# w_mod's load as two 64-row halves, one on SyncE's queue and one on ScalarE's

## The chip, the core and the metric

The kernel runs on one core of a Trainium2 chip. The core has a matrix engine (TensorE, PE in the profile; its weight loads are PEld), VectorE (DVE), ScalarE (ACT), GpSimd (POOL) and SyncE (SP), which here only issues transfers. Transfers between the chip's memory (HBM) and the core's on-chip memory of 128 rows (partitions) run on 16 DMA engines. The metric is device time in microseconds (us), the median of several runs.

## What is computed

One token of 640 numbers, x, goes through a transformer block with adaptive layer norm. A vector c gives six modulation vectors: silu(c) times w_mod, a matrix of 640 x 3840. Then comes attention with a cache of 32 heads, 16,384 keys and values of 128 numbers for each, and then a gated feed-forward layer. All arrays are bf16.

```
mod = (silu(c) @ w_mod).reshape(1, 6, 1, 640)
sa, ca, ga, sb, cb, gb = six rows of mod
h = layernorm(x) * (1 + ca) + sa
q = h @ wq                      # 32 heads of 128
p = softmax(q k^T / sqrt(128))  # 16384 keys a head
x = x + ga * ((p v) @ wo)
h = layernorm(x) * (1 + cb) + sb
x = x + gb * ((silu(h @ w_gate) * (h @ w_up)) @ w_down)
```

Nearly all bytes are the two caches, 16 pairs of heads with 8.39 MB of keys (K) and as much of values (V) each. w_mod has 4.92 MB and wq 5.24 MB; the whole input is 290.5 MB.

## The kernel before, in words

The kernel is a list of operations, each with an engine, a position (a number that sorts the operations of one engine), and the operations that it depends on. A small planner (lines 38 to 180) sorts each engine's list by position and writes it out. An engine works its list strictly in order; before an operation it waits on the semaphores of those that it depends on. Transfers are operations too (line 71): one instruction on an engine that issues it, by default SyncE, and a semaphore that is raised when the transfer has landed. Transfers that one engine issues stand in one queue.

**On-chip memory.** One large buffer, `big`, has three slots of 65,536 bytes a row. w_mod lies in slot 2 and wq in slot 1 (lines 237 and 238) until they are used up; K of pair 0 goes to slot 0, K of pair 1 to slot 1, V to slot 2. So K of pair 1 may be loaded only when the q matmuls have read all of wq (line 485), and V of pair 0 only when the w_mod matmuls are done (line 615).

**The queues at the start.** SyncE issues w_mod (line 327), wq (line 328), K of pair 0 in two halves of 4.19 MB (line 484), then K of pair 1 and V of pair 0, and from there on a K and a V for each turn of the loop over pairs, each waiting for its slot to come free. ScalarE issues c and x (lines 325 and 326), 1,280 bytes each. `w_mod.rearrange("(p k) n -> p k n", p=128)` puts five rows of w_mod side by side into each on-chip row, so an on-chip row takes 38,400 contiguous bytes.

**What uses them.** In PE's order: c is turned into columns (line 344), then x (line 345); VectorE and ScalarE make silu(c) (lines 348 to 351). PE makes the sums of the layer norm (lines 370 and 377), the partition number from a ramp that VectorE writes after `xn` (lines 353 to 361), x in chunks (line 346), and then the rows of the modulation (`mod_rows`, line 405): for shift and scale (line 415), and for five further banks (line 423), three of them before the first q matmul. VectorE picks columns out of them (`take`, line 398) and makes `h_col` (line 422). The q matmuls (lines 435 to 457) run in eight groups, each copied out by ScalarE (line 450).

**The loop over pairs.** VectorE multiplies K by q in place (line 627), folds halves together (line 640), and sums (line 642) to get the scores; ScalarE makes the exponentials (line 562); PE multiplies them with V (line 578). In the last pair PE takes over an eighth of the scores. At the end come wo, the second layer norm, and the feed-forward layer, whose weights are loaded in the slots that are free by then (lines 662 to 703).

Of the kernel before, what the change touches and what calls it, by code (L numbers as in the profile page):

```python
# [37 lines left out]
class _Plan:  # L38
# [21 lines left out]
    def op(self, eng, pos, fn, deps=(), name="", chan=None, turn=None):  # L60
        o = _Op(eng, pos, fn, list(deps), name, len(self.ops))
        o.turn = turn
        if chan is not None:
            if chan not in self.chans:
                self.chans[chan] = _Chan(self.es.enter_context(self.nc.semaphore("ch_" + chan)), 1)
            o.chan = self.chans[chan]
            o.sig = True
        self.ops.append(o)
        return o
# [113 lines left out]
def build(nc, A_x, A_k, A_v, A_wq, A_wo, B_wg, B_wu, B_wd, c_in, w_mod, out):  # L183
# [33 lines left out]
    with es:  # L217
        block = es.enter_context(nc.Block())
        plan = _Plan(nc, es)
# [15 lines left out]
        def mat(n, o, k, cols):  # L235
            return slot(n)[:, o:o + k * cols].rearrange("p (k n) -> p k n", k=k)
        wm_v = mat(2, 0, KC, 6 * D)
# [76 lines left out]
        ACT, DVE, PE = "act", "dve", "pe"  # L314
        op = plan.op
# [7 lines left out]
        wm_src = w_mod.rearrange("(p k) n -> p k n", p=128)  # L323
        wq_src = A_wq.rearrange("(p k) n -> p k n", p=128)
        d_c = plan.dma(0.06, c_one, c_in, "c", name="dma_c", eng="act")
        d_x = plan.dma(0.07, x_one, A_x[0], "x", name="dma_x", eng="act")
        d_wm = plan.dma(0.0, wm_v, wm_src, "wm", name="dma_wmod")
        d_wq = plan.dma(0.1, wq_v, wq_src, "wq", name="dma_wq")


# [20 lines left out]
        o_sc = op(DVE, 0.5, lambda e: e.tensor_tensor(out=silu_c[:], in0=c_col, in1=rr[:], op=ALU.mult), deps=[o_rr], name="silu_c")  # L351
# [3 lines left out]
        while n < 128:  # L355
            o_rp = op(DVE, 1.3 + 0.001 * n, lambda e, n=n: e.tensor_scalar_add(out=ramp[:, n:2 * n], in0=ramp[:, 0:n], scalar1=float(n)),
                      deps=[o_rp], name="ramp%d" % n)
            n *= 2
        o_pc = op(PE, 1.5, lambda e: e.matmul(A_ps[:, 0:1], lhsT=ramp[0:1, :], rhs=one_f[0:1, 0:1], start=True, stop=True),
                  deps=[o_rp, o_onesf], name="partition_number")  # L360
        o_pn = op(DVE, 1.6, lambda e: e.tensor_copy(out=on_f[:, 0:1], in_=A_ps[:, 0:1]), deps=[o_pc], name="partition_number_sb")
        o_ident = op(DVE, 1.7, lambda e: e.tensor_scalar(out=ident[:], in0=ramp, scalar1=on_f[:, 0:1], scalar2=None, op0=ALU.is_equal),
                     deps=[o_pn], name="ident")
# [41 lines left out]
        def mod_rows(pos, dst, c0, c1, deps, name):  # L405
            def f(e):
                last = None
                for a in range(c0, c1, 512):
                    b = min(a + 512, c1)
                    for kd in range(KC):  # L410
                        last = e.matmul(dst[:, a - c0:b - c0], lhsT=silu_c[:, kd:kd + 1].broadcast_to([128, 128]), rhs=wm_v[:, kd, a:b],  # L411
                                        start=(kd == 0), stop=(kd == KC - 1))
                return last
            return op(PE, pos, f, deps=[d_wm, o_sc] + deps, name=name)
        for m, (wide, free) in enumerate(((psw[3], o_rstd), (psw[2], o_pn))):
            o_m = mod_rows(2.0 + 0.01 * m, wide, m * D, (m + 1) * D, [free], "mod_rows%d" % m)
            for k in range(KC):
                take(2.05, wide[:, k:D:KC], moda[:, m * KC + k:m * KC + k + 1], o_m)
        o_t1 = op(DVE, 2.1, lambda e: e.scalar_tensor_tensor(
            out=tt1[:], in0=moda[:, KC:2 * KC], scalar=1.0, in1=xn[:], op0=ALU.add, op1=ALU.mult),  # L420
            deps=[o_take[-1], o_xn], name="t1")
        o_h = op(DVE, 2.2, lambda e: e.tensor_tensor(out=h_col[:], in0=tt1[:], in1=moda[:, 0:KC], op=ALU.add), deps=[o_t1], name="h_col")
        mod_banks = [6, 7, 4, 5, 2]
        for i, bk in enumerate(mod_banks):
            late = i >= 3
            o_mod_b = mod_rows((2.52 if late else 2.4) + 0.001 * i, psb[bk], 2 * D + 512 * i, 2 * D + 512 * (i + 1), [o_take[2 * KC - 1]], "mod_rows_b%d" % i)
            for c in range(4):
                o_modc = take(BU(0) + 4.2 if late else 2.42, psb[bk][:, 128 * c:128 * (c + 1)], modb[:, 4 * i + c:4 * i + c + 1], o_mod_b)
# [182 lines left out]
        for u in range(NU):  # L611
# [13 lines left out]
            for c, (a, b) in enumerate(zip(cuts, cuts[1:])):  # L625
                qb = qbc[:, u].unsqueeze(1).broadcast_to([128, b - a, 128])
                prev.append(op(DVE, B + (13.0 if u == 0 else 4.5) * c, lambda e, ks=ks[:, a:b, :], qb=qb: e.tensor_tensor(out=ks, in0=ks, in1=qb, op=ALU.mult),  # L627
                               deps=[d_k[u][c if u == 0 else 0], o_qbc[u]], name="mult%d_%d" % (u, c)))
# [9 lines left out]
            while w > 16:  # L638
# [4 lines left out]
                          deps=prev + ([o_exp[u - 1]] if u else []) + [o_xs.get(u)], name="red%d" % u)  # L643
            o_max[u] = op(DVE, E - 0.5, lambda e, u=u: e.tensor_reduce(out=pm[:], in_=S_v[:], axis=AX.X, op=ALU.max),  # L644
                          deps=[o_red[u], o_row[u - 1] if u else None], name="max%d" % u, chan="max")
# [56 lines left out]
        for a in range(2 * NP2, FCH):  # L702
# [5 lines left out]
                  deps=[o_abf, o_modc], name="ga_attn")  # L708
        o_x1 = op(DVE, TE + 0.2, lambda e: e.scalar_tensor_tensor(
            out=x1, in0=tt2[:], scalar=1.0, in1=x_res[:], op0=ALU.mult, op1=ALU.add, accum_out=st[:, 4:5]),  # L710
            deps=[o_ga, o_xf1], name="x1")
# [3 lines left out]
            deps=[o_xc1, o_rstd1, o_onep_b], name="t2")  # L715
        o_h2 = op(DVE, TE + 1.1, lambda e: e.tensor_tensor(out=h2_col[:], in0=tt3[:], in1=sb_, op=ALU.add),
                  deps=[o_t2], name="h2_col")
# [5 lines left out]
        def f_hrow(e):  # L723
            last = None
            for c in range(KC):
# [5 lines left out]
                   deps=[o_hr], name="h2_row1")]  # L731
# [34 lines left out]
        for i, (a, b) in enumerate(zip(WD_CUTS, WD_CUTS[1:] + [FCH])):  # L766
# [13 lines left out]
            deps=[prev, o_gbx, o_x1, o_zf], name="out_pairs")  # L780
# [9 lines left out]
def bass_adaLN_cond__gqa_block_cached__swiglu_ffn__decode_kernel(  # L790
    nc: bass.Bass,
    A_x: bass.AP,
    A_k_cache: bass.AP,
    A_v_cache: bass.AP,
    A_wq: bass.AP,
    A_wo: bass.AP,
    B_x: bass.AP,
    B_w_gate: bass.AP,
    B_w_up: bass.AP,
    B_w_down: bass.AP,  # L800
    c: bass.AP,
    w_mod: bass.AP,
    out: bass.AP,
):
    build(nc, A_x, A_k_cache, A_v_cache, A_wq, A_wo, B_w_gate, B_w_up, B_w_down, c, w_mod, out)
# [28 lines left out]
```

## Time and profile before

| | us |
|---|---|
| median of 3 runs (lowest and highest) | 681.05 (680.98 to 681.2) |
| the profiled execution | 681.08 |
| its span, from first to last instruction | 679.2 |
| VectorE busy in the span | 613.4 |
| TensorE busy in the span | 172.2 |
| ScalarE busy in the span | 59.7 |
| bytes moved by DMA, mean rate | 290.61 MB, 428 GB/s |

The profile is one execution of the kernel, as the hardware's profiler recorded it. A page of it gives busy times, the span cut into 40 slices with a digit for the busy share of each engine in tenths, the queues, and the costliest groups of instructions. The trace behind it can be asked further. A row of its timeline reads: start, duration (both us), engine, line of the kernel, operation, what is written <- what is read, how many; then in brackets the time for which the engine had been idle before, and what ended that. SPq and ACTq are instructions by which SyncE and ScalarE issue transfers; their duration is that of the issue and not of the transfer. For every packet that a DMA engine moved the trace has a record with queue, start, duration and bytes; a table of queues adds them up.

| issues at the start | issued at us | KB | us from issue to landing |
|---|---|---|---|
| w_mod, SyncE | 0.73 | 4800 | 14.1 |
| c, ScalarE | 0.76 | 1.2 | |
| wq, SyncE | 1.20 | 5120 | 26.1 |
| x, ScalarE | 1.31 | 1.2 | |
| K of pair 0, two halves, SyncE | 1.65 on | 4096 each | 40.4 (median) |

### The profile page before, as it was taken

The page shows a single profiled execution, that of the slowest core. Times are in us where ns is not written, and L with a number is a line of the kernel's source. Part 1 is how long each engine was busy: PE and PEld are TensorE (multiplying, and loading weights), DVE is VectorE, ACT ScalarE, POOL GpSimd, SP SyncE. Part 2 cuts the span into 40 slices and gives each one's busy share as a digit, 9 for nine tenths or more (in the row PEclk, how much of TensorE's full clock was granted, in tenths as well). Part 3 has the DMA queues.
Part 4 walks back from the last instruction along what each step waited for, and adds up shares of the span by engine and source line. Part 5 has one row for each costly group of instructions (what it writes and reads, how often), then busy time and mean ns, then how long its engine had stood idle before and what let it go on. Part 6 is the DMA issues. An engine that isn't in the chain of part 4 may idle for free.

```text
span 679.2 us, 4346 instructions
## 1 busy us (share of the span) xinstructions
PE 172.2 (25%) x1840; PEld 85.9 (13%) x1840; DVE 613.4 (90%) x250; ACT 59.7 (9%) x203; POOL 0.2 (0%) x4
## 2 busy tenths in 40 slices
PE   2720040404013030403103040301204030213465
PEld 1300010201001010201001010100101010102244
DVE  2389999999999999999999999999999999999801
ACT  1120100101010100101010100001010100003110
POOL 0000000000000000000000000000000000000000
PEclk9975565755557575655757565565756565566675
DMA  9999999999999999999999999999999999999996
GB/s 384 429 458 432 432 432 436 432 432 432 432 433 432 432 432 432 432 432 432 432 432 436 429 432 432 432 436 432 432 432 432 432 432 436 432 436 438 423 422 280
DMA packets 6936, 290.61 MB, mean 428 GB/s; under 512 B 716, under 2 KB 910, under 8 KB 1678
## 3 DMA queue, kind: packets, MB, share of 16 engines
q1 hardware_dynamic: 6922, 290.48, 99.1%
q8 instruction: 6, 0.10, 0.1%
q14 instruction: 4, 0.03, 0.0%
q10 hardware_dynamic: 4, 0.00, 0.0%
HBM read 290.47 MB, written 0.00 MB: 428 GB/s over the span
## 4 chain that ended last, share of the span: by engine, by line
DVE 80%; DMA 14%; issue 3%; SPq 2%; PE 0%
DVE big L627 35%; DVE big L640 33%; DMA big<-in_A_k_cache_dram 11%; DVE S_v L642 10%; DMA big<-in_B_w_down_dram 3%; SPq L78 2%; DVE big L630 1%; DVE gm L548 0%; DVE pm L644 0%; DVE on_f L595 0%; DVE kt L400 0%; PE psw L772 0%; DVE acc_sb L400 0%; DVE psw L488 0%; DVE S_v L400 0%
## 5 line engine op out<-in xcount | busy, mean ns | idle before, releaser
L627 DVE TENSOR_TENSOR big<-big,qbc 128x8192 bf16<-128x8192 bf16 (+3 forms) x32 | 275.5, 8610 | 13.1 <-DMA big<-in_A_k_cache_dram 13.1
L640 DVE TENSOR_TENSOR big<-big 128x8192 bf16<-128x8192 bf16 (+5 forms) x47 | 236.0, 5021 | 1.6
L578 PE MATMUL psw<-big,P 128*8 128x512 bf16 x1024 | 90.2, 529 | 114.4 <-DMA big<-in_A_v_cache_dram 114.4
L545 PE MATMUL psw<-ident_f,pm 128*1 128x128 f32 x32 | 9.4, 396 | 267.4 <-DVE pm L644 267.4
L642 DVE TENSOR_REDUCE S_v<-big 128x256 f32<-128x4096 bf16 (+1 forms) x16 | 70.2, 4387 | 0.5
L578 PEld LDWEIGHTS psw<-big,P 128*8 128x8 bf16 x1024 | 29.3, 111 | 168.6 <-DMA big<-in_A_v_cache_dram 111.7
L545 PEld LDWEIGHTS psw<-ident_f,pm 128*1 128x1 f32 x32 | 1.4, 80 | 269.2 <-DVE pm L644 269.2
L558 ACT ACTIVATE nb<-psw 128x1 f32<-128x1 f32 x16 | 2.7, 171 | 361.0 <-PE psw L555 361.0
L582 ACT ACTIVATE acc_sb<-psw 128x512 f32<-128x512 f32 x16 | 9.6, 597 | 191.6 <-PE psw L578 191.6
L555 PE MATMUL psw<-gm,one_f 1*64 1x1 f32 x64 | 6.0, 251 | 62.0 <-DVE gm L548 62.0
L589 PE MATMUL psw<-sel,acc_sb 128*128 128x2 f32 x128 | 16.8, 253 | 10.3 <-ACT acc_sb L582 10.3
L562 ACT ACTIVATE P<-S_v,nb 64x256 bf16<-64x256 f32 x32 | 18.5, 578 | 0.7
L589 PEld LDWEIGHTS psw<-sel,acc_sb 128*128 128x128 f32 x128 | 15.5, 191 | 17.5 <-ACT acc_sb L582 17.5
L567 PE MATMUL psw<-rs,one_f 128*128 128x2 f32 x32 | 9.2, 357 | 23.5 <-ACT P L562 23.5
L555 PEld LDWEIGHTS psw<-gm,one_f 1*64 1x64 f32 x64 | 4.6, 200 | 70.1 <-DVE gm L548 70.1
L595 DVE TENSOR_TENSOR on_f<-psw,rl 128x2 f32<-128x2 f32 x16 | 2.4, 153 | 11.2 <-PE psw L589 11.2
L411 PE MATMUL psw<-big,silu_c 128*128 128x512 bf16 (+1 forms) x45 | 10.6, 401 | 3.3 <-DMA big<-in_w_mod_dram 2.1
L567 PEld LDWEIGHTS psw<-rs,one_f 128*128 128x128 f32 x32 | 7.8, 304 | 25.2 <-ACT P L562 24.7
L443 PE MATMUL psw<-big,h_col 128*128 128x512 bf16 x40 | 9.0, 379 | 3.0 <-DMA big<-in_A_wq_dram 3.0
L400 DVE SCALAR_TENSOR_TENSOR kt<-psw,ident_f 128x128 f32<-128x128 f32 x20 | 4.7, 287 | 4.7 <-PE psw L411 4.4
L630 DVE TENSOR_TENSOR big<-big 128x8192 bf16<-128x8192 bf16 x2 | 8.8, 4417 | 0.0
L600 ACT ACTIVATE Z<-msk,on_f 128x16 bf16<-128x16 f32 x32 | 7.9, 293 | 1.1 <-DVE on_f L595 1.0
(102 smaller groups left out, 102.5 us busy)
## 6 DMA issues: line engine op xcount, KB each, us to landing
big<-in_A_k_cache_dram SPq DMA_DIRECT2D x2, 4096.0 KB, 40.4
big<-in_A_wq_dram SPq DMA_DIRECT2D x1, 5120.0 KB, 26.1
big<-in_w_mod_dram SPq DMA_DIRECT2D x1, 4800.0 KB, 14.1
big<-in_A_wo_dram SPq DMA_DIRECT2D x1, 3840.0 KB, 22.4
big<-in_B_w_gate_dram SPq DMA_DIRECT2D x1, 2160.0 KB, 23.1
big<-in_B_w_up_dram SPq DMA_DIRECT2D x1, 2160.0 KB, 27.9
big<-in_A_wo_dram SPq DMA_DIRECT2D x1, 1280.0 KB, 25.0
big<-in_B_w_down_dram SPq DMA_DIRECT2D x1, 960.0 KB, 29.9
```

The lines of the kernel that those rows point to most:

```text
L78: return e.dma_start(out_ap, in_ap)
L411: last = e.matmul(dst[:, a - c0:b - c0], lhsT=silu_c[:, kd:kd + 1].broadcast_to([128, 128]), rhs=wm_v[:, kd, a:b], start=(kd == 0), stop=( ...
L545: o_row[u] = op(PE, pos, lambda e: e.matmul(row_ps, lhsT=pm[:], rhs=ident_f[:], start=True, stop=True), deps=dv, name="row%d" % u, turn=tu ...
L555: last = e.matmul(top_ps[64 * hh:64 * hh + 64, :], lhsT=one_f[0:1, :].broadcast_to([1, 64]), rhs=gm2[:, hh:hh + 1], start=True, stop=True)
L562: o_exp[u] = op(ACT, pos + 0.03 + 0.01 * hh, lambda e, p_=p_, hh=hh: e.activation(out=P2[p_, :, hh], in_=S_v[p_, :], func=ACTF.Exp, scale= ...
L567: o_L = op(PE, pos, lambda e: e.matmul(L_ps, lhsT=ones_f, rhs=rs[:], start=True, stop=True), deps=[o_exp[u]], name="L%d" % u, turn=turn_of ...
L578: last = e.matmul(acc_ps[32 * (m % 4):32 * (m % 4) + 8, :], lhsT=P2f[:, 8 * m:8 * m + 8], rhs=vt[:, 512 * m:512 * (m + 1)], start=(m < 4), ...
L589: last = e.matmul(OT_ps, lhsT=acc_sb[:, 128 * i:128 * (i + 1)], rhs=sel[:, 2 * i:2 * i + 2], start=(i == 0), stop=(i == 3))
L627: prev.append(op(DVE, B + (13.0 if u == 0 else 4.5) * c, lambda e, ks=ks[:, a:b, :], qb=qb: e.tensor_tensor(out=ks, in0=ks, in1=qb, op=ALU ...
L630: prev[c] = op(DVE, B + 13.0 * c + 8.7, lambda e, ks=ks[:, a:b, :]: e.tensor_tensor(out=ks[:, :, 0:64], in0=ks[:, :, 0:64], in1=ks[:, :, 6 ...
L640: prev = [op(DVE, E - 14.0 + 0.1 * (8 - math.log2(w)), lambda e, ks=ks[:, 0:nt, :], w=w: e.tensor_tensor(out=ks[:, :, 0:w], in0=ks[:, :, 0 ...
L642: o_red[u] = op(DVE, E - 4.0, lambda e, ks=ks, nt=nt: e.tensor_reduce(out=S_v[:, 0:nt], in_=ks[:, 0:nt, 0:16], axis=AX.X, op=ALU.add), dep ...
```

## The change

The load of w_mod becomes two. Rows 0 to 63 of the on-chip slot are loaded by SyncE at the place of the old load, and rows 64 to 127 by ScalarE, with a semaphore of its own, at position 0.04: ahead of ScalarE's activation table load (0.05) and of its two other transfers, c (0.06) and x (0.07). The matmuls that read w_mod wait for both halves. Nothing else in any engine's order changes. A row keeps its 38,400 bytes, and all bytes together stay as they were.

```diff
         d_c = plan.dma(0.06, c_one, c_in, "c", name="dma_c", eng="act")
         d_x = plan.dma(0.07, x_one, A_x[0], "x", name="dma_x", eng="act")
-        d_wm = plan.dma(0.0, wm_v, wm_src, "wm", name="dma_wmod")
+        d_wm = plan.dma(0.0, wm_v[0:64], wm_src[0:64], "wm", name="dma_wmod0")
+        d_wm2 = plan.dma(0.04, wm_v[64:128], wm_src[64:128], "wm2", name="dma_wmod1", eng="act")
         d_wq = plan.dma(0.1, wq_v, wq_src, "wq", name="dma_wq")
...
-            return op(PE, pos, f, deps=[d_wm, o_sc] + deps, name=name)
+            return op(PE, pos, f, deps=[d_wm, d_wm2, o_sc] + deps, name=name)
```

## The prediction

> **What bounds the kernel now.** I read the page's slices first, then the waits, then the timeline at three places: the start, the first turn of the loop, the last two turns. From the page:
>
> ```profile
> span 679.2 us, 4346 instructions
> PE 172.2 (25%) x1840; PEld 85.9 (13%) x1840; DVE 613.4 (90%) x250; ACT 59.7 (9%) x203; POOL 0.2 (0%) x4
> ...
> DMA  9999999999999999999999999999999999999996
> ```
>
> VectorE is busy for 90% of the span, and the DMA engines are busy in every one of the 40 slices. Which of the two sets the end is told by the table of stretches (busy time of each engine, then granted clock, DMA share, GB/s) and by two rows of the timeline near the end:
>
> ```profile
> 47.00:308.00 261.00, 50.83 (x482) 22.28 (x482) 259.73 (x70) 16.33 (x58) 0.00 (x0) 0.56 1.00 434
> 308.00:570.00 262.00, 57.60 (x560) 25.75 (x560) 260.26 (x63) 19.52 (x70) 0.00 (x0) 0.58 1.00 433
> ...
> 570.20 4.42 DVE L627 TENSOR_TENSOR big<-big,qbc 128x8192 bf16<-128x8192 bf16 x1 [0.74 <-DMA big<-in_A_k_cache_dram]
> 608.89 4.42 DVE L627 TENSOR_TENSOR big<-big,qbc 128x8192 bf16<-128x8192 bf16 x1 [0.73 <-DMA big<-in_A_k_cache_dram]
> ```
>
> VectorE needs 37.87 us for a pair of heads (308.87 to 346.74 in the chain). One pair brings 16.78 MB, which at 433 to 434 GB/s is 38.7 us. So the transfers are slower than VectorE by 0.8 us a pair; they start with a lead, and VectorE has used it up at pair 14, where it waits 0.74 us for K, and again 0.73 us at pair 15. From there the end hangs on the bytes. The DMA share is 1.00 from 47 to 645 us, so nothing is made up on the way: **a microsecond lost by the transfers before 47 us is a microsecond at the end**. A microsecond won is worth at most about 1.5 us in all (those two waits), unless VectorE starts earlier too, as it does when K's first half lands earlier.
>
> The start, from the timeline, with the idle time before each and what ended it:
>
> ```profile
> 0.73 0.41 SPq L78 DMA_DIRECT2D big<-in_w_mod_dram  x1
> 0.76 0.51 ACTq L78 DMA_DIRECT2D kt<-in_c_dram  x1
> 1.31 0.21 ACTq L78 DMA_DIRECT2D qbc<-in_A_x_dram  x1
> ...
> 7.32 0.35 PE L338 MATMUL psw<-one_bf,qbc 1*128 1x1 bf16 x5 [4.89 <-DMA qbc<-in_A_x_dram]
> ...
> 14.86 4.89 PE L411 MATMUL psw<-big,silu_c 128*128 128x512 bf16 x20 [2.11 <-DMA big<-in_w_mod_dram]
> ...
> 27.37 1.25 PE L443 MATMUL psw<-big,h_col 128*128 128x512 bf16 x5 [2.96 <-DMA big<-in_A_wq_dram]
> ...
> 37.06 8.69 DVE L627 TENSOR_TENSOR big<-big,qbc 128x16384 bf16<-128x16384 bf16 x1 [11.68 <-DMA big<-in_A_k_cache_dram]
> 38.73 0.81 SPq L78 DMA_DIRECT2D big<-in_A_v_cache_dram  x1
> ```
>
> PE waits for x, for w_mod, for wq; VectorE waits 11.68 us for K. All of these follow SyncE's queue, which carries w_mod, wq and K one behind the other.
>
> **Part 1, the load itself.** Before, the trace's DMA records show w_mod as 128 packets of 38,400 B: on each of 16 engines 8 packets of 1.42 us, one starting as the other ends, with the first about 2.1 us long; the last ends at 14.56 us. That is 27.0 GB/s an engine, 11.36 us in all. wq (40,960 B in 1.514 us), the first K (32,768 B in 1.213 us) and later loads (65,536 B in 2.415 us) give 27.0 to 27.1 as well. So the limit is in bytes, but the records can't tell whether it is the engine's or that of the eight rows that it writes, since in a 128-row load each engine has eight rows of its own.
>
> After, each half has 64 rows: 4 packets an engine and queue (the one 64-row load of before, the last of w_down, shows 4 an engine). Two engines now share what one had in a half. Bounds: if the limit is the engine's, nothing is lost (0 us). If it is the rows', and all 16 engines write the same half at once, each packet takes twice as long, and w_mod costs another 11.36 us. The nearest rows are those of w_down's 64-row load: most of its 1,280 B packets take 55 ns as in a 128-row load, one engine's four take 85, 69, 73 and 68, so either end is in them. But the engines reach that load as much as some 2 us apart, with 0.21 us of work each; two that share rows are seldom in it at once. In w_mod all 16 start within 0.87 us of each other, with packets of 1.42 us, both queues are there from the start, and engines that alternate between them stay in step. I take the upper end, less what the stagger saves: two starts taken at random are 0.15 us apart in the median, a tenth of a packet, so a packet takes about 1.9 times, not 2: 0.9 x 11.36 = **10.2 us**. Being first on ScalarE's queue hides no part of it; SyncE's queue is the path, and wq and K stand behind.
>
> [...]
>
> **Part 2, c and x.** They now stand behind 4 packets an engine on ScalarE's queue, each landing as a data packet and a 4-byte one. Before, x's data went at 5.53 us and its 4 bytes at 6.99 us, one packet of SyncE's queue between them: the two queues alternate on an engine. So after ScalarE's half come wq, c, wq, c's 4 bytes, wq, x, wq, x's 4 bytes: x lands four wq packets (4 x 1.514 = 6.1 us) after w_mod. At full rate that is 14.0 + 6.1 = 20.1 us on that engine instead of 7.3; with part 1 about 30.7.
>
> What follows x, from the timeline: x's columns, both sums, the ramp, partition number, x's chunks, to 12.76 us, 5.4 us after 7.32; w_mod's rows to the third late group, 14.86 to 24.41, 9.6 us; then the q matmuls, 27.36 to 38.33, 11.0 us (paced by ScalarE's copies), after which SyncE may issue K for pair 1 into wq's place, and V behind it. Sum 26.0 us from x to that issue. The waits for w_mod (2.11) and wq (2.96) go; x is late instead. At full rate K would be issued at 46.1 and its packets start 1.1 us later (0.73 to 1.82 for w_mod), at 47.2. The engines run dry of K's pair 0 between 45.15 and 46.97 by their records. The slowest, which decides a landing, would stand 0.2 us. With part 1: issue at 56.7, packets at 57.8, slowest engine dry at 46.97 + 10.2 = 57.2: **0.6 us** idle. VectorE's first multiply needs pair 0's q, 17.1 us after x: 47.8, beside K's landing at 37.06 + 10.2 = 47.3, so the work is hidden to within half a microsecond, and VectorE has a lead on K of pair 1. c's chain (1.2 us to silu) ends before x lands.
>
> **Part 3, the rest.** One DMA issue more on ScalarE (0.4 to 0.5 us, ahead of a table load of 1.28 us and of two issues, nothing of which is needed before c lands); one semaphore more for PE's wait, which ends earlier than x's chain: 0. No other engine's order changes. Two sequencers starting at once could fill the queues sooner; the first packets start between 1.82 and 2.69, so at most some 0.5 us is to be won.
>
> **Sum.** Profiled execution 681.08 us (span 679.2 and 1.9 around it; the median of the three runs is 681.05). 681.08 + 10.2 + 0.6 = **691.9 us**, 1.6% slower.
>
> **Rivals.**
> Full rate: the limit is the engine's, and the halves take 11.4 us together. Then c and x are late but hidden, and the slowest engine stands 0.2 us; with the engines brought level at 47.2 and a stray instruction fetch up to 0.7 us: 681.2 to 682, no change, so not slower. For it: the 55 ns packets of w_down's 64-row load. Against: the shared rows. It decides when packets keep to 1.42 us. [...]
> Half of it: the engines that share rows fall into opposite halves, one on ScalarE's packet while the other is on SyncE's, after a start more than half a packet apart (0.7 us; the spread is 0.87). Then 1.2 to 1.6 times: 684 to 688.
> A longer dry spell: x's first packet of before waited for two packets of SyncE's queue, not one. If each of the four waits is two packets, x lands 6 us later, the engines stand idle up to 6 us on top of part 1: 694 to 698.
> A gain from the earlier start: 680.6.
>
> **Chances.** Forecast (689 to 694) 0.60; full rate 0.23; half of it 0.09; longer dry spell 0.06; gain 0.02. About 0.2% (1.4 us) is what a measurement of this kernel can tell from no change. Faster 0.02, within 0.2% 0.22 (nearly all of full rate), slower 0.76. To leave out no more than 2 in 10, the range must take in full rate at its lower end: 681.0 to 694.5. The forecast's own range is 689 to 694.
>
> **What would show it.** Right: w_mod's packets near 2.7 us; its landing near 25 us; x's matmuls near 31, SyncE's first V near 57; VectorE's first K multiply near 47.5; everything behind shifted by one amount to the last. Wrong: w_mod landed by 15 us and x by 20 (full rate); or the first multiply late by 10 us and the end not, which would mean that the transfers have slack that I didn't see.

## The result, and the profile after

The change makes the kernel slower: 696.38 us (median of 5 runs, 696.22 to 696.48) against 681.03 us beside it (5 runs, 680.86 to 681.2). The ratio is 1.0225, with a 95% interval of 1.0214 to 1.0236: 15.35 us more, where 10.8 were forecast and 13.5 was the end of the range.

From the pages of both kernels, first the GB/s line of before:

```profile
GB/s 384 429 458 432 432 432 436 432 432 432 432 433 432 432 432 432 432 432 432 432 432 436 429 432 432 432 436 432 432 432 432 432 432 436 432 436 438 423 422 280
```

Then the changed kernel: the span, the busy share of the DMA engines and the GB/s in 40 slices of 17.4 us, and ScalarE's queue, which is q10 (packets, MB, share of the 16 engines' span):

```profile
span 694.6 us, 4347 instructions
...
DMA  9998999999999999999999999999999999999997
GB/s 212 333 427 339 423 423 464 442 423 423 423 426 468 434 423 423 423 460 442 426 423 423 423 468 434 426 423 423 453 445 426 426 423 423 464 438 420 430 402 286
...
q10 hardware_dynamic: 84, 2.46, 1.6%
```

Two slices tell two different things. In the first the engines are marked busy at little more than half the rate (212 GB/s, before 384): they work, but slowly. In the fourth they have a dent in their busy share (8) and 339 GB/s: there they stand. What is behind runs at the old rate (433 GB/s from 69.5 to 650 us, as from 47 to 645 us before).

The table of stretches has both. Its columns are the stretch, then busy times, then granted clock, DMA share and GB/s. Before the change:

```profile
14.60:30.00 15.40, 10.94 (x48) 4.84 (x49) 5.42 (x46) 0.76 (x2) 0.00 (x0) 1.00 1.00 430
...
47.00:61.00 14.00, 0.00 (x0) 0.00 (x0) 13.86 (x10) 0.00 (x0) 0.00 (x0) 0.50 1.03 445
```

After it:

```profile
14.60:30.00 15.40, 0.00 (x0) 0.00 (x0) 0.00 (x0) 0.00 (x0) 0.00 (x0) 1.00 0.97 285
...
47.00:61.00 14.00, 12.24 (x57) 5.20 (x55) 12.59 (x38) 6.04 (x16) 0.00 (x0) 1.00 0.89 362
```

From 14.6 to 30 us the DMA share is 0.97 at 285 GB/s, and no engine of the core does anything at all: they wait for c, which stands behind ScalarE's half. From 47 to 61 us the share is 0.89.

The timeline shows what the core waited for, and that the end still hangs on K:

```profile
0.73 0.54 SPq L78 DMA_DIRECT2D big<-in_w_mod_dram  x1
0.73 0.56 ACTq L78 DMA_DIRECT2D big<-in_w_mod_dram  x1
...
30.17 0.35 PE L339 MATMUL psw<-one_bf,kt 1*128 1x1 bf16 x5 [30.17 <-DMA kt<-in_c_dram]
...
33.26 0.35 PE L339 MATMUL psw<-one_bf,qbc 1*128 1x1 bf16 x5 [2.73 <-DMA qbc<-in_A_x_dram]
...
38.62 5.18 PE L412 MATMUL psw<-big,silu_c 128*128 128x512 bf16 x20
...
50.44 8.69 DVE L628 TENSOR_TENSOR big<-big,qbc 128x16384 bf16<-128x16384 bf16 x1 [1.01 <-ACT qbc L451]
...
59.65 0.43 SPq L78 DMA_DIRECT2D big<-in_A_v_cache_dram  x1
...
584.82 4.43 DVE L628 TENSOR_TENSOR big<-big,qbc 128x8192 bf16<-128x8192 bf16 x1 [0.74 <-DMA big<-in_A_k_cache_dram]
...
623.51 4.42 DVE L628 TENSOR_TENSOR big<-big,qbc 128x8192 bf16<-128x8192 bf16 x1 [0.73 <-DMA big<-in_A_k_cache_dram]
```

x is read at 33.26 us, not 7.32; the w_mod matmuls (38.62) have no wait in brackets, so w_mod is no longer what they wait for. V is issued at 59.65 us, right behind K of pair 1. VectorE's waits for K at pairs 14 and 15 are the same 0.74 and 0.73 us as before, only 14.6 us later: it is still the transfers that set the end.

The DMA records (one for each packet) give the lost time. Steady w_mod packets take 2.79 us (those of ScalarE's half 2.80) instead of 1.42. The order on the engine that carries c and x, by queue, is S S A S A S A A, then wq, ScalarE's closing 4 bytes, wq, c, wq, c's 4 bytes, wq, x, wq, x's 4 bytes (S and A are the packets of SyncE's and ScalarE's half). The first K packet starts at 37.15 us instead of 25.80, and the last of pair 0 ends at 57.75 instead of 46.98. K of pair 1 starts at 60.23 on the first engine and 61.04 on the last (before: 45.17 and 46.98, without a gap), and its 16 first packets take 3.10 us in the median instead of 2.42.

| place | before | after | later by |
|---|---|---|---|
| K of pair 0, last packet ends | 46.98 | 57.75 | 10.8 |
| K of pair 1, last engine starts | 46.98 | 61.04 | 14.1 |
| pair 15, VectorE's first multiply | 608.89 | 623.51 | 14.6 |
| wo matmuls start | 656.89 | 672.25 | 15.4 |
| end of the span | 679.2 | 694.6 | 15.4 |

### The profile page after: what moved, and what is told of

Its sections match the earlier page's. It is cut to its first block, busy times and chain, and to the rows that moved or that the text cites. A ratio compares the mean times of both kernels' runs of the same rounds, so it can differ in the third digit from the quotient of the medians.

```text
span 694.6 us, 4347 instructions
## 1 busy us (share of the span) xinstructions
PE 173.8 (25%) x1840; PEld 86.6 (12%) x1840; DVE 613.5 (88%) x250; ACT 59.7 (9%) x203; POOL 0.2 (0%) x4
## 4 chain that ended last, share of the span: by engine, by line
DVE 73%; DMA 19%; issue 3%; SPq 2%; PE 2%; ACT 0%; ACTq 0%; DVEq 0%
DVE big L628 32%; DVE big L641 30%; DMA big<-in_A_k_cache_dram 11%; DVE S_v L643 9%; DMA qbc<-in_A_x_dram 4%; DMA big<-in_B_w_down_dram 3%; SPq L78 2%; DVE big L631 1%; PE psw L412 1%; DVE gm L549 0%; DVE kt L401 0%; DVE acc_sb L357 0%; PE psw L444 0%; DVE on_f L596 0%; DVE acc_sb L401 0%
## 5 line engine op out<-in xcount | busy, mean ns | idle before, releaser
L590 PEld LDWEIGHTS psw<-sel,acc_sb 128*128 128x128 f32 x128 | 15.5, 191 | 17.4 <-ACT acc_sb L583 17.4
L596 DVE TENSOR_TENSOR on_f<-psw,rl 128x2 f32<-128x2 f32 x16 | 2.4, 153 | 12.9 <-PE psw L590 12.9
```

The lines of the kernel that those rows point to most:

```text
L590: last = e.matmul(OT_ps, lhsT=acc_sb[:, 128 * i:128 * (i + 1)], rhs=sel[:, 2 * i:2 * i + 2], start=(i == 0), stop=(i == 3))
```

## The experiments

The theory: two 64-row halves make all 16 engines write the same half of the rows, which takes twice as long; and c and x, behind ScalarE's half, delay the q matmuls and with them K of pair 1, so that the engines stand. Rivals: alternating between two queues is slow in itself; or the slow part is made up later and the order is the whole loss; or it is the reading side of the memory that is slow. All diffs are against the changed kernel; where loads of w_mod are shown as added lines alone, they stand in place of the two lines `d_wm` and `d_wm2` of the change. Each experiment ran beside the kernel before the change (681.10 to 681.14 us).

**1. Rows, c and x ahead of ScalarE's half.**

```diff
-        d_wm2 = plan.dma(0.04, wm_v[64:128], wm_src[64:128], "wm2", name="dma_wmod1", eng="act")
+        d_wm2 = plan.dma(0.08, wm_v[64:128], wm_src[64:128], "wm2", name="dma_wmod1", eng="act")
```

> The two 64-row halves on two queues as in the change, but c and x issued ahead of ScalarE's half. Theory: the loss of 15.3 us has two parts, about 11 us from packets of a 64-row half that take twice as long (2.79 us instead of 1.42 in the trace), and about 4 us because x lands at 33 us, K for pair 1 is issued at 59.2 us and the engines stand idle. Then only the first part is left here: packets still near 2.79 us, x landed by some 15 us, no idle DMA engines before 60 us, 691.5 to 692.5 us. Rival, order alone: the slow packets would be made up elsewhere and the late x would be the whole loss, then 681 to 683 us.

Measured: 694.31 us, ratio 1.019 (1.0173 to 1.0207). The engines never stand (K of pair 1 starts within 3 ns of the end of pair 0 on the last engine), so the order's part is gone, and the rival "order alone" falls. But 13.2 us are left, not 11. The records have the rest: ScalarE's half now starts late, its last packets run beside wq, and wq's packets are longer as well: 43 of its 128 packets are longer than 1.6 us, up to 3.8, against 15 in the changed kernel, up to 2.1. They cost 2.5 us an engine here, 0.4 there.

**2. and 3. Columns instead of rows, c and x behind or ahead.** Both queues carry all 128 rows, half of each row's bytes.

```diff
-        d_wm = plan.dma(0.0, wm_v[0:64], wm_src[0:64], "wm", name="dma_wmod0")
-        d_wm2 = plan.dma(0.04, wm_v[64:128], wm_src[64:128], "wm2", name="dma_wmod1", eng="act")
+        wm_f, wm_s = slot(2)[:, 0:WM_E], w_mod.rearrange("(p k) n -> p (k n)", p=128)
+        d_wm = plan.dma(0.0, wm_f[:, 0:WM_E // 2], wm_s[:, 0:WM_E // 2], "wm", name="dma_wmod0")
+        d_wm2 = plan.dma(0.04, wm_f[:, WM_E // 2:WM_E], wm_s[:, WM_E // 2:WM_E], "wm2", name="dma_wmod1", eng="act")
```

Experiment 3 has 0.08 in place of 0.04.

> w_mod cut by columns instead: both queues carry a load of all 128 rows with 19,200 bytes a row, and c and x stay behind ScalarE's half as in the change. Theory (shared rows): packets of 19,200 bytes in 0.71 us, full rate, w_mod landed near 15 us; x lands five wq packets (7.6 us) later, near 22.5 us; K for pair 1 is issued 26.0 us after that, at 48.6 us, and starts near 49.7 us, against engines that run dry between 45.2 and 47.0 us: 2.7 us idle for the slowest and 0.5 us for the restart, 684 to 685 us. Rival, two queues that alternate are slow whatever they carry: packets twice as long, 692 us or more.

> w_mod cut by columns over both queues, c and x ahead of ScalarE's half. Theory (shared rows, late x): neither cost is left, 680.7 to 681.5 us, as before the change. Rival, alternating queues are slow: about 692 us.

Measured: 683.9 us behind (ratio 1.0041, 1.0027 to 1.0056), 681.11 us ahead (1.0001, 0.9991 to 1.001). Packets of 19,200 bytes take 0.714 us, full rate. So two queues cost nothing, and a late x alone costs 2.8 us. In the profiled execution of experiment 2 (682.33 us, the shortest of its five; the others had 683.6 to 684.25) ScalarE's packets came first on the engines, x landed at 18.6 us, and the last engine stood only 0.2 us. That the others had SyncE's packets first, and x one wq packet (1.5 us) later, would fit the difference, but no trace of them shows it.

**4. Both row halves on SyncE's queue.**

```diff
-        d_wm2 = plan.dma(0.04, wm_v[64:128], wm_src[64:128], "wm2", name="dma_wmod1", eng="act")
+        d_wm2 = plan.dma(0.01, wm_v[64:128], wm_src[64:128], "wm2", name="dma_wmod1")
```

> The two 64-row halves one behind the other on SyncE's queue, ScalarE's queue as before the change. Theory (shared rows): all 16 engines write the same half at once whether one queue or two carry it, packets near 2.8 us, w_mod landed near 26 us, c and x early, 691.5 to 692.5 us. Rival, alternating queues are slow: packets at 1.42 us, 681 us.

Measured: 693.64 us, ratio 1.0184 (1.0167 to 1.0201), packets of 3.00 us. One queue is no better: the rows do it. It is even worse than two queues in step (2.79 us), by 7%, which I had not expected.

**5. and 6. Four loads of 32 rows; eight of 16 rows.** One behind the other on SyncE's queue. Experiment 6 has 16 in place of 32.

```diff
+        d_wms = [plan.dma(0.001 * i, wm_v[i:i + 32], wm_src[i:i + 32], ("wm", i), name="dma_wmod%d" % i) for i in range(0, 128, 32)]
...
-            return op(PE, pos, f, deps=[d_wm, d_wm2, o_sc] + deps, name=name)
+            return op(PE, pos, f, deps=d_wms + [o_sc] + deps, name=name)
```

> w_mod as four loads of 32 rows, one behind the other on SyncE's queue; ScalarE's queue as before the change. Theory A, the rate goes with the number of rows that a load covers: 32 rows give a quarter of it, packets near 5.7 us, w_mod takes 45 us instead of 11.4, 681 + 34 = 715 us. [...]

> w_mod as eight loads of 16 rows, one behind the other on SyncE's queue. Theory A (rate in proportion to the rows): an eighth, packets near 11.4 us, w_mod takes 91 us, about 760 us. [...]

Measured: 693.31 us with 32 rows (ratio 1.0178, 1.0161 to 1.0195), packets of 2.99 us, no slower than with 64; 715.43 us with 16 rows (1.0509, 1.0491 to 1.0526), packets of 5.27 us. The rate doesn't go with the number of rows (theory A had 5.7 and 11.4 us a packet). 32 rows are as good as 64 (2.99 against 3.00 us), 16 rows give a little over half of that rate. Against the 1.42 us of the 128-row load, packets take 2.1, 2.1 and 3.7 times as long on one queue with 64, 32 and 16 rows. Why it goes in these steps no run shows.

**7. Even and odd rows on two queues, c and x ahead.**

```diff
+        d_wm = plan.dma(0.0, wm_v[0:128:2], wm_src[0:128:2], "wm", name="dma_wmod0")
+        d_wm2 = plan.dma(0.08, wm_v[1:128:2], wm_src[1:128:2], "wm2", name="dma_wmod1", eng="act")
```

> SyncE's load takes the even rows, ScalarE's the odd rows, 64 rows each, and c and x go ahead of ScalarE's load. Theory C, what halves the rate is that a load stays in one half of the rows: these loads spread over all 128, so packets at 1.42 us, 681 us. [...]

Measured: 681.48 us (ratio 1.0004, 0.9995 to 1.0014), packets of 1.42 us. Theory C is right here: 64 rows that are spread over all 128 run at full rate. The number of rows is not what counts, nor that a load is one of two. ScalarE's late half runs beside wq here too, and no wq packet takes more than 1.52 us (in experiment 1 up to 3.8): what slowed wq there is the rows as well.

**8., 9. and 10. Which side, and does it need two queues?** 8 spreads only the on-chip rows, 9 only the rows of the memory, 10 has even and odd rows one behind the other on SyncE's queue. In 8 and 9 w_mod's rows lie on chip in another order than the matmuls take them, so these two are for timing alone: they leave out the right modulation and have all of its work.

```diff
+        d_wm = plan.dma(0.0, wm_v[0:128:2], wm_src[0:64], "wm", name="dma_wmod0")
+        d_wm2 = plan.dma(0.08, wm_v[1:128:2], wm_src[64:128], "wm2", name="dma_wmod1", eng="act")
```

```diff
+        d_wm = plan.dma(0.0, wm_v[0:64], wm_src[0:128:2], "wm", name="dma_wmod0")
+        d_wm2 = plan.dma(0.08, wm_v[64:128], wm_src[1:128:2], "wm2", name="dma_wmod1", eng="act")
```

```diff
+        d_wm = plan.dma(0.0, wm_v[0:128:2], wm_src[0:128:2], "wm", name="dma_wmod0")
+        d_wm2 = plan.dma(0.01, wm_v[1:128:2], wm_src[1:128:2], "wm2", name="dma_wmod1")
```

> Only the on-chip side is spread: SyncE's load writes the even rows from the first half of w_mod's memory, ScalarE's the odd rows from the second half, c and x ahead. w_mod's rows stand in another order, so the modulation is computed with other values, at the same cost. Theory D, what is shared is on the on-chip side: packets at 1.42 us, 681 to 681.6 us. Rival S, reading 64 neighbouring rows of the memory is what is slow: packets near 2.8 us, 693.5 to 694.5 us.

> Only the memory side is spread: SyncE's load writes on-chip rows 0 to 63 from w_mod's even rows, ScalarE's rows 64 to 127 from its odd rows, c and x ahead; again the modulation is computed with rows in another order. Theory D (on-chip side): packets near 2.8 us, 693.5 to 694.5 us as with the halves and c and x ahead. Rival S (memory side): packets at 1.42 us, 681 to 681.6 us.

> Even rows, then odd rows, both on SyncE's queue, so all engines work on one kind at a time. Theory E, 64 rows spread over all 128 reach as much as 128 do: packets at 1.42 us, 681 to 681.6 us. Rival, even and odd rows together were full only because two queues complemented each other: packets near 2.8 us, 692.5 to 694 us.

Measured: 8: 681.51 us (ratio 1.0005, 0.9996 to 1.0015), 1.42 us a packet. 9: 693.97 us (1.0191, 1.0174 to 1.0208), 2.73 us. 10: 681.5 us (1.0005, 0.9995 to 1.0015), 1.42 us. The lists of transfers (KB, us from issue to landing) have it in two lines each. With the on-chip rows spread:

```profile
big<-in_w_mod_dram SPq DMA_DIRECT2D x1, 2400.0 KB, 13.2
big<-in_w_mod_dram ACTq DMA_DIRECT2D x1, 2400.0 KB, 16.6
```

With only the memory's rows spread:

```profile
big<-in_w_mod_dram SPq DMA_DIRECT2D x1, 2400.0 KB, 22.6
big<-in_w_mod_dram ACTq DMA_DIRECT2D x1, 2400.0 KB, 29.1
```

The same bytes in the same packets land 9 to 13 us apart. These two differ in both sides, but with experiments 1 and 7 all four cases are there: with blocks of on-chip rows the load is slow whether the memory's rows are a block (1) or spread (9), and with spread on-chip rows it is at full rate either way (8 and 7). So it is the on-chip rows.

**11. The change with c and x on GpSimd's queue.**

```diff
-        d_c = plan.dma(0.06, c_one, c_in, "c", name="dma_c", eng="act")
-        d_x = plan.dma(0.07, x_one, A_x[0], "x", name="dma_x", eng="act")
+        d_c = plan.dma(0.06, c_one, c_in, "c", name="dma_c", eng="pool")
+        d_x = plan.dma(0.07, x_one, A_x[0], "x", name="dma_x", eng="pool")
```

> The change with c and x on GpSimd's queue, so that ScalarE's half starts at once, in step with SyncE's, and x stands behind nothing. Theory: the change minus the idle time of the engines, that is a shift of about 10.7 to 11.3 us and none of the 2 us by which the halves with c and x ahead on ScalarE fell out of step and slowed wq: 691.7 to 692.7 us; wq's packets near 1.5 us. Rival: whatever goes ahead, the halves cost 13 us, then 694 us.

Measured: 692.62 us, ratio 1.0168 (1.0151 to 1.0185). The size is right; that x "stands behind nothing" is not. In the timeline x is read at 26.48 us, and in the table of stretches the engines don't stand all the same:

```profile
26.48 0.35 PE L339 MATMUL psw<-one_bf,qbc 1*128 1x1 bf16 x5 [7.96 <-DMA qbc<-in_A_x_dram]
```

```profile
47.00:61.00 14.00, 5.72 (x26) 2.27 (x25) 12.19 (x19) 4.64 (x13) 0.00 (x0) 0.88 1.03 444
```

A DMA share of 1.03 at 444 GB/s, where the change had 0.89 at 362. So x may come 19 us later than before at no cost, if w_mod is late too; 7 us more, and it costs 3.8 us: the change's 15.35 less the 11.5 that are left here.

**The sum over all kernels.** For each kernel I added up, over the DMA records to 95 us, what each packet of w_mod, wq and K took beyond the steady time of its size (0.714, 1.42, 1.514, 1.213 and 2.415 us), divided by 16 engines, and took off the same sum of the kernel before (0.76 us). "Idle" is from the last end of K of pair 0 to the last engine's start on K of pair 1. Packet times are medians. "Measured" is the median less that of before; for experiment 2, whose runs differ, it is that of the profiled execution.

| kernel | w_mod packet, us | longer packets | idle | sum | measured |
|---|---|---|---|---|---|
| the change | 2.80 | 11.7 | 3.3 | 15.0 | 15.35 |
| 1 rows, c and x ahead | 2.85 | 13.1 | 0 | 13.1 | 13.2 |
| 2 columns, c and x behind | 0.714 (half) | 0.7 | 0.2 | 0.9 | 1.2 |
| 3 columns, c and x ahead | 0.714 (half) | 0.0 | 0 | 0.0 | 0.0 |
| 4 rows, one queue | 3.00 | 12.1 | 0 | 12.1 | 12.5 |
| 5 32 rows | 2.99 | 12.2 | 0 | 12.2 | 12.2 |
| 6 16 rows | 5.27 | 31.6 | 2.3 | 33.9 | 34.3 |
| 7 even and odd rows | 1.42 | 0.0 | 0 | 0.0 | 0.3 |
| 8 on-chip rows spread | 1.42 | 0.2 | 0 | 0.2 | 0.4 |
| 9 memory rows spread | 2.73 | 12.5 | 0 | 12.5 | 12.9 |
| 10 even and odd, one queue | 1.42 | -0.1 | 0 | -0.1 | 0.4 |
| 11 rows, c and x on GpSimd | 2.77 | 11.3 | 0 | 11.3 | 11.5 |

In every row the first microseconds give the end to within 0.5 us. Most of what is left has a place of its own: in all eight kernels with 64-row loads, those of spread rows too, SyncE's first issue takes 0.54 to 0.56 us and w_mod's first packet starts at 2.05 to 2.08 us; in the others, the kernel before among them, the issue takes 0.40 to 0.41 us and the packet starts at 1.74 to 1.76 us. These 0.3 us are not in the sum; with them, all rows but 2 and 6 come within 0.2 us. That is what "the transfers never stand" means: a loss there is never made up. No version here beats the kernel before the change.

## Why the prediction was wrong, step by step

- **What bounds the kernel:** right. The loss at the start stood at the end in every kernel of the table, and in the change VectorE's waits for K stayed at 0.74 and 0.73 us.
- **Part 1, the load:** right in mechanism, a little short. Packets take 1.97 times as long, not 1.9: the stagger of the starts saved next to nothing (the 16 engines started within 0.49 us of each other, before within 0.87). The load cost 11.5 us (experiment 11) instead of 10.2: w_mod's own packets lost 10.6 there, wq's, the first of them still beside w_mod's last, 0.6, and the late start 0.3. "If it is the rows'" is now shown for the on-chip rows (experiments 8 and 9). That an engine's eight rows are the unit isn't: 32 rows cost no more than 64 (2.99 and 3.00 us a packet).
- **Part 2, c and x:** this is the step that failed, at "**0.6 us** idle". Measured 3.3 us of idle engines and 0.5 to 0.7 us of longer first packets at the restart, about the 3.8 us between the change and experiment 11. The chain from x to K's issue was right (33.26 to 59.27 us is 26.0, as forecast). Its start was not: x was read at 33.3 us, not 30.7. 1.1 us of it came from part 1 (w_mod's end and wq's first packet), 1.5 us from a fifth wq packet: SyncE's queue got two packets in before ScalarE's first, so ScalarE's closing 4 bytes stood behind a wq packet as well. I had counted four waits and left out the one of the half's own closing record. The restart was forecast too early as well: 1.1 us from issue to packets is the first engine's delay, and the engine that decides is the last, which started 1.8 us after the issue (before, w_mod's last engine had started 1.9 us after its issue). So 0.6 us becomes 3.3: 2.6 more for x, 0.7 for the last engine, less 0.6 by which pair 0's K itself ended later than forecast. The restart's longer packets were no term of the sum at all. The sum compared two numbers 0.6 us apart, each uncertain by more: the slack was used up, so every further microsecond of x counted in full, and I put too little of the range there. The rival "a longer dry spell" (694 to 698 us) has the time that came, but not by its mechanism: it had two packets in each of four waits, and there was one packet in each of five. Nor were the two sums for x started alike: 46.1 counts from its landing (20.1), 56.7 from its reading (30.7, which is 0.4 more than 20.1 + 10.2). Started alike, the case of full rate has some 0.6 us of idle engines, not 0.2.
- **Part 3, the rest:** put at 0, and it cost 0.3 us. SyncE's issue of its half took 0.54 us, before 0.41 for the whole, and the first packets start at 2.05 us, before at 1.76 (the prediction read 1.82); that goes through to the end. ScalarE's issue of c got longer too (0.90 us, before 0.51), which cost nothing.
- **Full rate, half of it, a gain:** none came. The 55 ns packets of w_down's last load, which spoke for full rate, were indeed too short and too far apart to tell.
- **14.6 us at pair 15, 15.4 at wo:** nothing was lost in between. By the mean of the 16 engines, K of pair 1 ends 15.5 us later, and every load from there to wo 15.4 to 15.5. Only the last engine, on which a landing waits, is 14.4 to 14.6 us later at first, because the pause had brought the engines level: they end K of pair 1 within 0.6 us, before within 1.9. Behind pair 15's K the spread grows again, to 1.8 us at wo (before 2.1), and the last engine is 15.4 us later too. PE starts 0.5 us behind wo's last packet in both kernels (656.35 and 656.89 us, 671.75 and 672.25).
- **Still open:** the records don't say which rows an engine writes in a load of even rows, so why 64 spread rows are full and 64 neighbouring ones are not is settled only as to the side. Why 32 neighbouring rows load as fast as 64 and 16 do not, why the restart's first packets are longer, why the issue of a 64-row load takes longer and why two queues are 7% quicker than one isn't shown either.

## What to carry to other kernels

If the DMA engines are busy to the end, a microsecond at the start is a microsecond at the end (here to within 0.5 us in every kernel), so cut a load in columns rather than in blocks of rows: for these 4.92 MB, columns cost nothing, even and odd rows 0.3 to 0.4 us, halves 11 to 13 us, eighths 34. A small transfer that others wait for goes ahead of a large one on its queue, with its closing record counted as a packet of its own; behind one, it costs what its slack doesn't cover (3.8 us in the change, 2.8 in experiment 2). Where a forecast finds a chain and its slack within a microsecond of each other, the range belongs on the far side.

## What the runs showed of the hardware that I had not expected

Two halves on two queues in step are 7% quicker a packet than on one queue (2.79 against 3.00 us). Packets of half the rows also slow full-width packets beside them: wq's from 1.51 up to 3.8 us in experiment 1 (in experiment 7, with even and odd rows, none is over 1.52). And 32 rows are as good as 64 (2.99 and 3.00 us), while 64 even rows are as good as 128 (1.42 us).
